# A planned attention-and-mixer kernel: transfers priced by packets, weights drawn forward, range check in two buffers

## The chip, the cores and the metric

The kernel runs on one core of one Trainium2 chip. The metric is the device time of one launch in microseconds, the median over several runs; lower is better. The engines are named as the profile names them: PE (matrix products, with PEld for loading their stationary side), DVE (vector), ACT (scalar), POOL and SP (which issues most DMAs).

## The reference

```
# attention: B, H, S, D = 4, 8, 768, 64; 16 centroids per head
q_n, k_n, c_n = (y / (norm(y) + 1e-6) for y in (q, k, centroids))
q_assign = argmax(q_n @ c_n.T);  k_assign = argmax(k_n @ c_n.T)
scores = where(q_assign == k_assign, q @ k.T / sqrt(D), -1e9)
attn_out = softmax(scores) @ v
# mixer on x = attn_out as (B, 768, 512); d_tok = 256, d_ch = 1536
h = relu(x.T @ w_tok1) @ w_tok2
u = x + h.T
out = u + relu(u @ w_ch1) @ w_ch2
```

q, k, v and the centroids are float32; the four weights come as float64, and the result is float32.

## The kernel before

The kernel first records every operation with its operands' places in one large SBUF tile (`arena`) and in PSUM (`ps`), and then a planner (`Program.run`, `Program.plan`) orders them. PE's operations keep the order in which they are recorded. For the other engines the planner keeps lists of operations whose predecessors are planned. At each step it takes, on the engine that can start soonest, the operation with the earliest due time among those that can start within `HOLD` of the first. Due times are worked backwards from PE's. Costs per engine are constants (`COST`, a cost given with `vec`), and a DMA occupies one shared bus for its bytes over `BUS` and lands `LAND` later. An operation with `after` isn't planned before that time. The order that comes out is written into each engine's queue; at run time each queue goes strictly in that order and waits on semaphores.

The work in PE's order:

- **Start.** Loads for the first pairs, the centroids' norm (`begin`), the first transposes by PE (`turn_qk`) and routing (`route`).
- **Attention.** 16 pairs of heads (`pair`). For each, `scores` makes 12 chunks of score products with a mask product added, ACT's exponential reads each chunk (line 1190), DVE adds the exponentials up (line 880), `sums` and `values` follow on PE, and `finish_x` transposes and scales the result on DVE (lines 1249 and 1263). `route` for the pair two ahead runs in between (DVE lines 1085 to 1090, ACT line 1094), and its mask goes through DRAM by two DMAs. The q and k of later pairs are turned by DMA transposes of 16-bit halves, with ACT copies on both sides (`part_qk`, `join_qk`, line 870).
- **Weights.** Beside attention the float64 weights are loaded in 31 pieces and rounded on DVE (`weight_round`, lines 1326, 1330, 1333, 1336 and a join on line 880). Piece n is not planned before `START + STEP * n`. The channel weights are combined for a seven-product scheme (two levels of it) and stored to DRAM (`wd1`, `wd2`) in 256-byte runs.
- **Token stage.** Seven-product forms of both token products (`token1`, `token2`). ACT copies halves for the transposes that bring x into u (`x_into_u`), and DVE adds PE's results.
- **Channel products.** `channel1` and `channel2`, each once for two batches (`grp` 0 and 1). Each calls `product` seven times, and each product reads seven weight tiles from DRAM into a ring of eight buffers, three matmuls to a tile. DVE or ACT copies take the results out of PSUM, and results go out by `send` and `store`.
- **Checks.** `weights_in_range` loads the raw weights again in 20 chunks of 768 KB into one buffer (`araw`), and ACT takes two sums of each (line 1863). `check` counts these, the softmax sums and the routing hits on DVE, adds them over partitions by one small matmul on PE, and makes a flag. `read_flag` loads the flag on every engine (line 1913). If it is not zero, `general_path` computes everything again; it is zero with these inputs.

A recorded operation carries the line of the helper that issues it: 841 for matmuls, 880 for two-operand adds, 860 for copies out of PSUM, 900 for DMAs.

Of the kernel before, what the change touches and what calls it, by code (L numbers as in the profile page):

```python
# [13 lines left out]
U32 = mybir.dt.uint32  # L14
ALU = mybir.AluOpType
ACT = mybir.ActivationFunctionType
# [14 lines left out]
HS = HJ * P  # L31
# [26 lines left out]
ISSUE = 0.63  # L58
BUS = 240e3
PASSES = 1  # L60
HOLD = {"DVE": 0.15}
WP = 768
NWP = (S * DTOK * 2 + DM * DCH * 2) // (P * WP)
LAND = 2.2
SWITCH = 0.1
SELF = 0.13
START, STEP = 14, 13


class Op:  # L70
    __slots__ = ("opts", "fn", "preds", "succs", "left", "ready", "end", "due", "seq", "eng", "lat", "bytes", "after", "port", "first_lat", "mode")


class Program:
# [7 lines left out]
    def __init__(self):  # L82
        self.ops, self.writer, self.readers = [], {}, {}

    def add(self, opts, fn, rd=(), wr=(), size=None, after=0.0, mode=None):

        o = Op()
        o.opts, o.fn, o.seq, o.succs, o.bytes, o.after = opts, fn, len(self.ops), [], 0, after
        o.lat, o.mode = 0.0, mode

        o.port = not any(type(k) is tuple and k[0] == "ps" for k in list(rd) + list(wr))
        if size:
            o.bytes = size[0] * (1.2 if size[1] < 512 else 1.0)
            o.lat = 5.0 + o.bytes / BUS
        o.first_lat = o.lat
        preds = set()
        for key in rd:
            if key in self.writer:
                preds.add(self.writer[key])
            self.readers.setdefault(key, []).append(o)  # L100
        for key in wr:
# [15 lines left out]
    def run(self):  # L117


        ops = self.ops  # L120

        free = 0.0
        for o in ops:
            c = min(o.opts.values())
            t = max([p.end + 0.15 + p.lat for p in o.preds], default=0.0)
            if "PE" in o.opts:
                t = max(t, free)
                free = t + c
            o.ready, o.end = t, t + c
        at = {o: o.ready for o in ops if "PE" in o.opts}  # L130
        total = max(o.end for o in ops)
        best = None
        for n in range(PASSES):

            for o in reversed(ops):
                c = min(o.opts.values())
                lat = o.first_lat
                if "PE" in o.opts:
                    o.due = at[o]
                else:  # L140
                    o.due = min([s.due - 0.15 - lat for s in o.succs], default=total) - c
            order, at, total = self.plan()
            if best is None or total < best[0]:
                best = (total, order)
        for o, e in best[1]:
            o.fn(e)

    def plan(self):
# [14 lines left out]
        while len(order) < len(ops):  # L163
            best = None
            for e in self.ENGINES:
# [5 lines left out]
                else:  # L171
# [548 lines left out]
def kernel(  # L720
# [27 lines left out]
    g = Program()  # L748
# [14 lines left out]
    at = 0  # L763

    def buf(kb, shape, dt=F32):
        return Buf(arena, int(kb * 256), shape, dt)
# [8 lines left out]
    cnt = Buf(arena, 352, [32])  # L775
    unsc = Buf(arena, 640, [2])
    low = Buf(arena, 644, [1])
    wsum = Buf(arena, 704, [2, NWP])
    araw = buf(75, [768, 2], U32)
    rcps = [Buf(arena, 384 + 32 * i, [2, NJ]) for i in range(2)]  # L780
    dall = Buf(arena, 448, [NP, 2, NJ])

# [7 lines left out]
    exs = [buf(48 + 6 * i, [2, S]) for i in range(6)] + [buf(96, [2, S])]  # L790
    es = [buf(84 + 6 * i, [2, S]) for i in range(2)]
    denT = buf(105, [HS])
    rt = [buf(106.5 + 1.5 * i, [HS]) for i in range(3)]

    qkr = buf(9, [2, 2, NJ, D])
# [39 lines left out]
    def bank(*i):  # L835
        return [("ps", n) for n in i]


    def mm(dst, lhsT, rhs, start, stop, cost, rd, wr, pos=None, tr=None):
        def fn(e):  # L840
            nc.tensor.matmul(  # L841
                dst, lhsT=lhsT, rhs=rhs, start=start, stop=stop, tile_position=pos,
                is_transpose=tr, skip_group_check=True,
            )

        return g.add({"PE": cost}, fn, rd, wr, mode=(lhsT.shape[0], lhsT.shape[1]))
# [43 lines left out]

        return g.add({e: cost(e, n) for e in engines}, fn, rd, wr)

    def vec(fn, c, rd, wr):
        return g.add({"DVE": c - 0.08}, lambda e: fn(), rd, wr)

    def dma(dst, src, rd, wr, kb, row, after=0.0, queue="SP"):

        q = {"SP": nc.sync, "ACT": nc.scalar, "POOL": nc.gpsimd}[queue]
        return g.add(
            {queue: ISSUE}, lambda e: q.dma_start(dst, src), rd, wr, (kb * 1024, row), after  # L900
        )

    def transpose(dst, src, rd, wr, kb):
        return g.add(
            {"SP": ISSUE}, lambda e: nc.sync.dma_start(dst, src, transpose=True), rd, wr,
            (1.3 * kb * 1024, 512),
        )


# [937 lines left out]
    def weights_in_range():  # L1847

        n = 0
        for w in (moe_w_tok1, moe_w_tok2, moe_w_ch1, moe_w_ch2):
            flat = w.rearrange("a b -> (a b)").rearrange("(p n) -> p n", p=P).bitcast(U32)
            for c in range(flat.shape[1] // (2 * WP)):
                dma(
                    araw.ap.rearrange("p n two -> p (n two)"),
                    flat[:, 2 * WP * c : 2 * WP * (c + 1)], [], araw.k(), 768, 6144, 430.0,
                )
                hi = araw.ap[:, :, 1].bitcast(F32)
                for i, (func, bias) in enumerate(((ACT.Square, 0.0), (ACT.Sign, low.ap))):  # L1860
                    g.add(
                        {"ACT": 0.9},
                        lambda e, i=i, func=func, bias=bias, n=n, hi=hi: nc.scalar.activation(  # L1863
                            out=hi, in_=hi, func=func, bias=bias, accum_out=wsum.ap[:, i, n : n + 1],
                        ),
                        araw.k() + low.k(), araw.k() + [("wsum", n)],
                    )
                n += 1

    def check():  # L1870
        n = NP * HJ * 4
        dv = dall.ap.rearrange("p m h j -> p (m h j)")
        ok = denT.ap[:, 0:n]
        rd = [("dall", m) for m in range(NP)]
        vec(lambda: nc.vector.tensor_scalar(
            out=ok, in0=dv, scalar1=SUM_LO, scalar2=None, op0=ALU.is_ge
        ), 0.3, rd, denT.k())
        vec(lambda: nc.vector.scalar_tensor_tensor(
            out=ok, in0=dv, scalar=SUM_HI, in1=ok, op0=ALU.is_le, op1=ALU.mult
        ), 0.3, rd + denT.k(), denT.k())  # L1880
        vec(lambda: nc.vector.reduce_sum(out=cnt.ap[:, 0:1], in_=ok, axis=AX.X), 0.3,
            denT.k(), cnt.k())
# [15 lines left out]
        vec(lambda: nc.vector.reduce_sum(  # L1898
            out=cnt.ap[:, 2:3], in_=wsum.ap, axis=AX.XY
        ), 0.2, wk, cnt.k())  # L1900
        mm(ps[0:32, 0, 0:3], ones.ap, cnt.ap[:, 0:3], True, True, 0.1,
           cnt.k() + ones.k(), bank(0), pos=(0, 0))
        tt(cnt.ap[0:1, 4:7], ps[0:1, 0, 0:3], want.ap[0:1], ALU.not_equal, 3,
           bank(0) + want.k(), cnt.k())
        vec(lambda: nc.vector.reduce_sum(
            out=cnt.ap[0:1, 7:8], in_=cnt.ap[0:1, 4:7], axis=AX.X
        ), 0.2, cnt.k(), cnt.k())
        vec(lambda: nc.vector.tensor_copy(
            out=cnt.ap[0:1, 8:9].bitcast(I32), in_=cnt.ap[0:1, 7:8]
        ), 0.2, cnt.k(), cnt.k())  # L1910
# [34 lines left out]
    left = [token2_sums(0)]  # L1945
# [17 lines left out]
    weights_in_range()  # L1963
    channel1(0)
    channel2(0)
    channel1(1)
    check()
    channel2(1)
    read_flag([])
    g.run()  # L1970
# [34 lines left out]
```

## Time and profile before

| | before |
|---|---|
| median of 3 runs | 803.17 us (802.9 to 803.7) |
| the profiled execution | 803.35 us, span 801.3 us, TensorE clock 0.998 |
| PE busy | 785.5 us, 98% of the span |
| DVE busy | 663.9 us, 83% |
| ACT busy | 468.0 us, 58% |
| POOL busy | 189.6 us, 24% |
| DMA | 264883 packets, 143.70 MB |

The span runs from the first to the last instruction; the profiled execution's own time has the launch around it. Busy times of matmuls are modelled and hold waits of a few tenths, so the distance between matmul records tells more than PE's share. The durations of single instructions overlap by up to a tenth of a microsecond with the next on their engine.

### The profile page before, as it was taken

To read this page: it belongs to the slowest core of one execution; us is meant where nothing else is said; L and a number is where in the kernel's file an instruction comes from. 1 tells how busy PE (TensorE), PEld (TensorE's weight loads), DVE (VectorE), ACT (ScalarE), POOL (GpSimd) and SP (SyncE) were. 2 spreads that over 40 slices of the span, in tenths; PEclk is the share of its full clock that TensorE was granted. 3 is DMA by queue.
4 is the path that set the end of the run, shared out by engine and by line. 5 is a ranking of instruction groups with operands and counts; after the bars stand their busy time and mean duration, and the time that the engine had idled before them with its cause. 6 is when DMAs were issued, how large, how long until landed. Compare 5 with 4: busy or idle time off the path is not lost.

```text
span 801.3 us, 15484 instructions
## 1 busy us (share of the span) xinstructions
PE 785.5 (98%) x6063; PEld 467.3 (58%) x6063; DVE 663.9 (83%) x863; ACT 468.0 (58%) x615; POOL 189.6 (24%) x185
## 2 busy tenths in 40 slices
PE   8999999999999999999999999999999999999995
PEld 5566666666666666544555555555555555555553
DVE  6888788999999999999998767899852677799962
ACT  5588888888888875699623235434537605401332
POOL 0000000000000000001255599700285289810000
PEclk9999999999999999999999999999999999999999
DMA  8466666998999875689967855557987943333765
GB/s 186 159 170 152 146 159 170 219 211 186 227 234 202 188 217 129 146 159 203 196 182 209 246 182 177 185 179 199 253 246 199 262 120 101 103 103 98 178 155 136
DMA packets 264883, 143.70 MB, mean 179 GB/s; under 512 B 184160, under 2 KB 260704, under 8 KB 264800
## 3 DMA queue, kind: packets, MB, share of 16 engines
q1 hardware_dynamic: 262432, 141.83, 70.0%
q8 instruction: 50, 0.82, 0.4%
q10 hardware_dynamic: 2368, 0.79, 0.4%
q14 instruction: 33, 0.27, 0.1%
HBM read 91.95 MB, written 28.61 MB: 150 GB/s over the span
## 4 chain that ended last, share of the span: by engine, by line
PE 83%; DVE 10%; ACT 4%; issue 2%; POOL 0%; DVEq 0%; POOLq 0%; ACTq 0%
PE ps L841 68%; PE ps L1207 15%; DVE arena L880 7%; ACT arena L870 2%; ACT arena L1190 1%; DVE arena L1330 1%; DVE arena L1333 0%; DVE arena L1263 0%; DVE arena L1336 0%; ACT arena L860 0%; ACT arena L887 0%; DVE arena L1326 0%; DVE arena L1249 0%; DVE arena L862 0%; DVE arena L1085 0%
## 5 line engine op out<-in xcount | busy, mean ns | idle before, releaser
L841 PE MATMUL ps<-arena 128*128 128x384 f32 (+5 forms) x2735 | 641.3, 462 | 7.9 <-DVE arena L862 2.1
L841 PEld LDWEIGHTS ps<-arena 128*128 128x128 f32 (+1 forms) x2351 | 341.5, 185 | 252.8 <-issue 58.6
L880 DVE TENSOR_TENSOR arena<-arena 128x256 f32<-128x256 f32 (+6 forms) x340 | 354.1, 1062 | 22.9 <-ACT arena L1190 14.2
L880 POOL TENSOR_TENSOR arena<-arena 128x384 f32<-128x384 f32 x179 | 188.9, 1085 | 514.8 <-DVE arena L880 390.9
L880 DVE TENSOR_TENSOR arena<-ps,arena 128x384 f32<-128x384 f32 (+3 forms) x227 | 189.1, 843 | 88.7 <-PE ps L841 85.2
L870 ACT COPY arena<-arena 128x768 uint16<-128x768 uint16 x223 | 191.4, 948 | 47.9 <-DMA arena<-arena 22.3
L1190 ACT ACTIVATE arena<-ps 128x768 f32<-128x768 f32 x192 | 153.0, 810 | 32.4 <-PE ps L841 30.7
L1207 PE MATMUL ps<-arena 128*32 128x192 f32 (+1 forms) x3328 | 151.1, 339 | 0.0
L1207 PEld LDWEIGHTS ps<-arena 128*32 128x32 f32 x3328 | 106.5, 110 | 48.0 <-issue 20.3
L860 ACT COPY arena<-ps 128x1152 f32<-128x1152 f32 (+2 forms) x42 | 30.8, 738 | 105.4 <-PE ps L841 105.4
L887 ACT ACTIVATE arena<-arena 128x1152 f32<-128x1152 f32 (+1 forms) x38 | 40.2, 1076 | 55.5 <-DVE arena L880 54.1
L1863 ACT ACTIVATE arena<-arena 128x768 f32<-128x768 f32 x40 | 38.8, 969 | 56.4 <-DMA arena<-in_moe_w_tok_dram 30.7
L841 PEld LDWEIGHTS <-arena 64*128 64x128 bf16 x384 | 19.2, 94 | 25.0 <-DVE arena L1117 0.6
L1094 ACT ACTIVATE arena<-arena 128x384 bf16<-128x384 f32 x16 | 11.3, 708 | 19.7 <-ACT arena L870 9.5
L1336 DVE SCALAR_TENSOR_TENSOR arena<-arena 128x512 f32<-128x512 uint32 (+1 forms) x31 | 21.2, 684 | 0.7
L1330 DVE SCALAR_TENSOR_TENSOR arena<-arena 128x512 uint32<-128x512 uint32 (+1 forms) x31 | 20.7, 669 | 0.8
L1263 DVE STREAM_TRANSPOSE arena<-ps 128x768 f32<-128x768 f32 x16 | 15.6, 975 | 1.1 <-PE ps L1207 1.0
L1333 DVE TENSOR_SCALAR arena<-arena 128x512 uint32<-128x512 uint32 (+1 forms) x31 | 14.2, 457 | 0.5
L1085 DVE STREAM_TRANSPOSE arena<-ps 128x384 f32<-128x384 f32 x16 | 9.3, 580 | 4.7 <-PE ps L841 4.6
L1326 DVE TENSOR_SCALAR arena<-arena 128x512 uint32<-128x512 uint32 (+1 forms) x31 | 12.5, 403 | 0.0
L1249 DVE STREAM_TRANSPOSE arena<-ps 128x384 f32<-128x384 f32 x16 | 9.2, 577 | 3.0 <-PE ps L1207 2.9
L1090 DVE STREAM_TRANSPOSE arena<-arena 128x384 f32<-128x384 f32 x16 | 9.3, 578 | 0.6
(58 smaller groups left out, 49.6 us busy)
## 6 DMA issues: line engine op xcount, KB each, us to landing
arena<-wd SPq DMA_DIRECT2D x196, 192.0 KB, 2.5
wd<-arena SPq DMA_DIRECT2D x84, 224.0 KB, 3.7
arena<-in_moe_w_ch_dram SPq DMA_DIRECT2D x48, 256.0 KB, 4.8
arena<-in_moe_w_ch_dram SPq DMA_DIRECT2D x16, 768.0 KB, 4.4
arena<-in_v_dram SPq DMA_DIRECT2D x16, 384.0 KB, 5.1
out_dram<-arena SPq DMA_DIRECT2D x14, 384.0 KB, 3.8
arena<-in_k_dram SPq DMA_DIRECT2D x13, 384.0 KB, 3.9
arena<-in_q_dram SPq DMA_DIRECT2D x13, 384.0 KB, 4.3
```

The lines of the kernel that those rows point to most:

```text
L841: nc.tensor.matmul(dst, lhsT=lhsT, rhs=rhs, start=start, stop=stop, tile_position=pos, is_transpose=tr, skip_group_check=True,)
L860: nc.scalar.copy(out=dst, in_=src)
L870: nc.scalar.copy(out=dst, in_=src)
L880: (nc.vector if e == "DVE" else nc.gpsimd).tensor_tensor(out=dst, in0=a, in1=b, op=op)
L887: nc.scalar.activation(out=dst, in_=src, func=ACT.Relu)
L1190: lambda e, ex=ex, s=s, u=u: nc.scalar.activation(out=ex.ap[:, :, u * HS : (u + 1) * HS], in_=ps[:, 2 * s : 2 * s + 2, 0:HS], func=ACT.Exp ...
L1207: nc.tensor.matmul(dst, lhsT=lhsT, rhs=rhs, start=start, stop=stop, tile_position=pos, skip_group_check=True,)
L1263: lambda: nc.vector.transpose(out=x.ap[:, :, cols].rearrange("p j (c d) -> p c j d", d=32), in_=ps[:, 6:8, 0:HS],),
L1330: vec(lambda: nc.vector.scalar_tensor_tensor(out=TT, in0=hi, scalar=0xC0000000, in1=hh, op0=ALU.bitwise_and, op1=ALU.bitwise_or), 0.14 + 0 ...
L1333: vec(lambda: nc.vector.tensor_scalar(out=hh, in0=TT, scalar1=0xFF800000, scalar2=None, op0=ALU.bitwise_and), f, T.k(), h.k())
L1336: vec(lambda: nc.vector.scalar_tensor_tensor(out=ll, in0=lo, scalar=float(2.0**-52), in1=hh.bitcast(F32), op0=ALU.mult, op1=ALU.mult,), 0. ...
L1863: lambda e, i=i, func=func, bias=bias, n=n, hi=hi: nc.scalar.activation(out=hi, in_=hi, func=func, bias=bias, accum_out=wsum.ap[:, i, n : ...
```

## The change

- A transfer's bytes on the planner's bus are now counted from its packets: 11 ns and 0.037 ns a byte for each run, over 16 DMA engines. DMA transposes are counted as 256-byte runs.
- ACT gets a `HOLD` of 0.2 us. DVE's stays at 0.15.
- `STEP` goes from 13 to 11 us, so piece n of the weights may be planned earlier.
- The range check of the weights alternates between two buffers (`araws`) and may begin at 418 us of the plan instead of 430.
- `check` uses a buffer of its own (`okb`) instead of `denT`, and is recorded ahead of `channel1(1)` instead of behind it, so that its matmul stands between the two groups in PE's order. The sum of the weights' counts gets a due time 20 us earlier (`early`).

```diff
-HOLD = {"DVE": 0.15}
+HOLD = {"DVE": 0.15, "ACT": 0.2}
...
-START, STEP = 14, 13
+START, STEP = 14, 11
...
         if size:
-            o.bytes = size[0] * (1.2 if size[1] < 512 else 1.0)
+            o.bytes = BUS * size[0] / size[1] * (11 + 0.037 * size[1]) / 16e3
             o.lat = 5.0 + o.bytes / BUS
...
-                    o.due = min([s.due - 0.15 - lat for s in o.succs], default=total) - c
+                    o.due = min([s.due - 0.15 - lat for s in o.succs], default=total) - c - o.early
...
-    araw = buf(75, [768, 2], U32)
+    araws = [buf(at, [768, 2], U32) for at in (75, 3)]
...
+    okb = buf(131.5, [HS])
...
     def transpose(dst, src, rd, wr, kb):
         return g.add(
             {"SP": ISSUE}, lambda e: nc.sync.dma_start(dst, src, transpose=True), rd, wr,
-            (1.3 * kb * 1024, 512),
+            (kb * 1024, 256),
         )
...
             for c in range(flat.shape[1] // (2 * WP)):
+                araw = araws[n % 2]
                 dma(
                     araw.ap.rearrange("p n two -> p (n two)"),
-                    flat[:, 2 * WP * c : 2 * WP * (c + 1)], [], araw.k(), 768, 6144, 430.0,
+                    flat[:, 2 * WP * c : 2 * WP * (c + 1)], [], araw.k(), 768, 6144, 418.0,
                 )
...
-        ok = denT.ap[:, 0:n]
+        ok = okb.ap[:, 0:n]
...
         vec(lambda: nc.vector.reduce_sum(
             out=cnt.ap[:, 2:3], in_=wsum.ap, axis=AX.XY
-        ), 0.2, wk, cnt.k())
+        ), 0.2, wk, cnt.k(), 20.0)
...
     weights_in_range()
     channel1(0)
     channel2(0)
+    check()
     channel1(1)
-    check()
     channel2(1)
     read_flag([])
```

More of the change, by code (lines that the diff above doesn't have):

```diff
@@ L66 @@
 SELF = 0.13
-START, STEP = 14, 13
+START, STEP = 14, 11
 class Op:
-    __slots__ = ("opts", "fn", "preds", "succs", "left", "ready", "end", "due", "seq", "eng", "lat", "bytes", "after", "port", "first_lat", "mode")
+    __slots__ = ("opts", "fn", "preds", "succs", "left", "ready", "end", "due", "seq", "eng", "lat", "bytes", "after", "port", "first_lat", "mode", "early")
 class Program:
@@ L83, in __init__, with add @@
         self.ops, self.writer, self.readers = [], {}, {}
-    def add(self, opts, fn, rd=(), wr=(), size=None, after=0.0, mode=None):
+    def add(self, opts, fn, rd=(), wr=(), size=None, after=0.0, mode=None, early=0.0):
         o = Op()
         o.opts, o.fn, o.seq, o.succs, o.bytes, o.after = opts, fn, len(self.ops), [], 0, after
-        o.lat, o.mode = 0.0, mode
+        o.lat, o.mode, o.early = 0.0, mode, early
         o.port = not any(type(k) is tuple and k[0] == "ps" for k in list(rd) + list(wr))
         if size:
-            o.bytes = size[0] * (1.2 if size[1] < 512 else 1.0)
+            o.bytes = BUS * size[0] / size[1] * (11 + 0.037 * size[1]) / 16e3
             o.lat = 5.0 + o.bytes / BUS
@@ L891, in relu, with vec @@
         return g.add({e: cost(e, n) for e in engines}, fn, rd, wr)
-    def vec(fn, c, rd, wr):
-        return g.add({"DVE": c - 0.08}, lambda e: fn(), rd, wr)
+    def vec(fn, c, rd, wr, early=0.0):
+        return g.add({"DVE": c - 0.08}, lambda e: fn(), rd, wr, early=early)
     def dma(dst, src, rd, wr, kb, row, after=0.0, queue="SP"):
@@ L1876, in check @@
             out=ok, in0=dv, scalar1=SUM_LO, scalar2=None, op0=ALU.is_ge
-        ), 0.3, rd, denT.k())
+        ), 0.3, rd, okb.k())
         vec(lambda: nc.vector.scalar_tensor_tensor(
             out=ok, in0=dv, scalar=SUM_HI, in1=ok, op0=ALU.is_le, op1=ALU.mult
-        ), 0.3, rd + denT.k(), denT.k())
+        ), 0.3, rd + okb.k(), okb.k())
         vec(lambda: nc.vector.reduce_sum(out=cnt.ap[:, 0:1], in_=ok, axis=AX.X), 0.3,
-            denT.k(), cnt.k())
+            okb.k(), cnt.k())
         vec(lambda: nc.vector.reduce_sum(out=cnt.ap[:, 10:11], in_=hits.ap[:, 0:NP], axis=AX.X), 0.2,
```

## The prediction

> **What bounds the kernel now.** I read the page's engine totals first, then busy time by stage, then the groups and waits of the stage that looked worst.
>
> ```profile
> span 801.3 us, 15484 instructions
> PE 785.5 (98%) x6063; PEld 467.3 (58%) x6063; DVE 663.9 (83%) x863; ACT 468.0 (58%) x615; POOL 189.6 (24%) x185
> PE 83%; DVE 10%; ACT 4%; issue 2%; POOL 0%; DVEq 0%; POOLq 0%; ACTq 0%
> ```
>
> TensorE is the bound, so the change can only win back time in which PE waits. A busy PE row includes stretched matmuls, so I count records against a full rate. The chain of waits shows that rate, and the period of one head pair in attention:
>
> ```profile
> 117.65 9.89 PE ps L841 x72
> 137.41 9.89 PE ps L841 x72
> ...
> 420.06 300.70 PE ps L841 x932
> ```
>
> The half with the channel products issues a 384-wide record every 300.70/932 = 0.323 us with hardly a gap; a 512-wide one should take 4/3 of that, 0.430 us. A head pair repeats every 137.41 - 117.65 = 19.76 us. Busy time by stage (columns: stretch, length, busy time and count of PE, PEld, DVE, ACT, POOL, then clock, DMA share, GB/s), and the token stage's matmul groups and waits:
>
> ```profile
> 180.00:200.00 20.00, 20.00 (x294) 12.54 (x292) 19.15 (x29) 17.38 (x23) 0.00 (x0) 1.00 0.84 189
> 220.00:240.00 20.00, 20.00 (x292) 12.44 (x290) 19.17 (x28) 17.38 (x23) 0.00 (x0) 1.00 0.95 232
> 333.60:421.00 87.40, 85.60 (x233) 42.62 (x230) 84.16 (x148) 61.39 (x77) 18.64 (x18) 1.00 0.86 183
> 421.00:621.00 200.00, 200.00 (x621) 117.42 (x620) 149.41 (x147) 88.21 (x129) 106.57 (x100) 1.00 0.72 207
> 720.00:760.00 40.00, 39.91 (x123) 22.68 (x121) 39.19 (x43) 9.25 (x13) 0.00 (x0) 1.00 0.58 141
> ...
> L841 PE MATMUL ps<-arena 128*128 128x384 f32 x145 | 49.0, 491 | 1.4 <-DVE arena L880 1.3
> L841 PE MATMUL ps<-arena 128*128 128x512 f32 x84 | 37.3, 598 | 0.4 <-ACT arena L860 0.2
> ...
> PEld ps L841 <- DVE arena L880: 6.8, 11, 1.2
> PEld ps L841 <- ACT arena L860: 2.6, 3, 1.0
> ```
>
> In the token stage (333.6 to 421) 145 x 0.323 + 84 x 0.430 = 82.9 us of matmuls took 87.4 us: PE loses 4.5 us there. DVE is busy 84.16 of 87.40 us, and of PE's weight-load waits 6.8 us are for DVE and 2.6 for ACT. In attention PE holds its period although DVE is at 19.2 of 20 us. So what can be won lies in the token stage, a little in the first 40 us, and a little at 720 to 760, where DVE is again full.
>
> **The change part by part.** Since all engines' order comes from the planner, I compare the order of the instructions before and after. PE's own order is unchanged but for the check's matmul and the flag load. All sums are against the profiled execution's 803.35 us (span 801.3); the median 803.17 is 0.02% below it, which I do not correct for.
>
> (1) STEP 11 for 13 draws the weights' rounding forward. One channel piece is four steps and a join, and its share of the product sums:
>
> ```profile
> L880 DVE TENSOR_TENSOR arena<-arena 128x448 f32<-128x448 f32 x48 | 29.7, 632 | 0.2
> L880 DVE TENSOR_TENSOR arena<-arena 128x512 f32<-128x512 f32 x35 | 24.5, 706 | 1.5 <-ACT arena L870 0.9
> L880 DVE TENSOR_TENSOR arena<-arena 128x256 f32<-128x256 f32 x48 | 19.4, 430 | 0.5
> L1336 DVE SCALAR_TENSOR_TENSOR arena<-arena 128x512 f32<-128x512 uint32 x27 | 19.0, 703 | 0.6
> L1330 DVE SCALAR_TENSOR_TENSOR arena<-arena 128x512 uint32<-128x512 uint32 x27 | 18.5, 686 | 0.7
> L1333 DVE TENSOR_SCALAR arena<-arena 128x512 uint32<-128x512 uint32 x27 | 12.8, 474 | 0.4
> L1326 DVE TENSOR_SCALAR arena<-arena 128x512 uint32<-128x512 uint32 x27 | 11.1, 413 | 0.0
> ```
>
> That is 0.41 + 0.69 + 0.47 + 0.70 + 0.71 = 2.98 us, and 2 x 0.43 + 2 x 0.63 = 2.12 us of sums: 5.1 us. By the order, 7 pieces stand behind the last pair's finish (L1263) before and 5 after, and none of the 5 in the channel products' time, where two stood. Two pieces, 10.2 us, leave DVE's queue between that finish and the first channel products; if nearly all of it is the token stage's, DVE has some 75 us to do there, not 84.2. DVE's part of the 4.5 us lost, by the waits 6.8/(6.8 + 2.6), is 3.2 us. I take four fifths, **-2.6 us**, since the middle of the stage still holds pieces; bounds 0 (ACT's copies are next late) and -3.8 (all but 0.7).
>
> The price is in attention. With the rows' durations (overlap with the next instruction taken off), DVE's work between two finishes of pairs 5 to 13 was 15.4 to 19.2 us and becomes 19.0, 19.0, 19.5, 19.2, 19.3, 20.0, 19.3, 19.8, 19.6: 19.4 on average, against 19.76. DVE keeps up by 0.4 us a pair; and the planner, which takes the earliest due step first, leaves the steps that free PE's banks ahead of rounding. I take **0**, up to +2 if it slips.
>
> The DMAs move too. The counting by packets (11 ns + 0.037 ns a byte) makes large rows cheaper and 256-byte transposes about 8% cheaper in the plan, so loads are planned to land earlier. In attention the weights' loads and stores come 13/11 as often, over a share of 0.84 to 0.95 already; the busiest pairs will be close to 1. [...]
>
> (2) The start is reordered by the new transfer prices.
>
> ```profile
> 20.23 0.71 ACT L1094 ACTIVATE arena<-arena 128x384 bf16<-128x384 f32 x1
> 21.77 0.30 PEld L841 LDWEIGHTS ps<-arena 64*128 64x128 f32 x4 [0.57 <-ACT arena L1190]
> ...
> 36.69 0.35 DVE arena L1333
> 37.06 0.69 DVE arena L1336
> 37.75 0.59 DVE arena L1085
> 38.38 10.10 PE ps L841 x72
> ```
>
> L1094 of pair 1 (0.71 us and its read) sat among pair 0's exponentials and PE waited behind it; it now comes after the tenth, when PE needs no more than two: about -0.35. At 36.69 two rounding steps stood ahead of L1085, which frees the bank that pair 1 starts in; now they come after it, and the third PSUM copy is ACT's. L1085 then starts when route's matmuls end, some 0.5 us sooner. Together **-0.85**, bounds -0.2 and -1.3 (the mask copies, shuffled too, could give some back).
>
> (3) The range check of the weights is drawn together.
>
> ```profile
> L1863 ACT ACTIVATE arena<-arena x40: 904/968/1031, 434.9 to 636.1; 128x768 f32<-128x768 f32 x40
> L1863 ACT ACTIVATION_READ_ACCUMULATOR arena<-arena x40: 182/190/198, 435.7 to 637.0; 128x1 f32 x40
> L860 ACT COPY arena<-ps 128x1152 f32<-128x1152 f32 x15 | 16.8, 1118 | 36.7 <-PE ps L841 36.7
> arena<-in_moe_w_ch_dram SPq DMA_DIRECT2D x16, 768.0 KB, 4.4
> ```
>
> A chunk costs ACT 2 x (0.97 + 0.19) = 2.3 us. In the order its 20 chunks stand over some 85 us of PE's matmuls instead of 200. ACT has room, but a range step ahead of a PSUM copy makes 1.16 + 1.12 = 2.28 us where a product step has 6 x 0.323 = 1.94: the second of two such copies is 0.7 us late, where its bank leaves 1.94 - 1.12 = 0.8 us less the handing over, an estimated 0.5. **+0.4**, bounds 0 and +1.5. On SP a chunk's load now waits for the chunk two earlier, with ring loads queued behind it; the ring is eight loads deep, some 15 us of PE work, so I price that at nothing; without that cover each wait would be PE's.
>
> (4) The counts. check's early sums go to its own buffer (okb) and run at the start of the channel products, off DVE's full stretch at 720 to 760; the matmul and the flag come at the seam of the two groups, where DVE is light. Every engine still loads the flag, so its queue still waits there.
>
> ```profile
> PEld ps L841 <- DVE arena L1908: 0.8, 1, 0.8
> ```
>
> The flag's weight-load wait was 0.8 us, of which a quieter DVE can save a part. I take **-0.3**, bounds -0.8 and +0.3. ACT's HOLD only lets a due step pass another by 0.2 us: nothing. The tail's order is the same except that one store is issued earlier: nothing.
>
> Sum: -2.6 + 0 - 0.85 + 0.4 - 0.3 = -3.35; 803.35 - 3.35 = **800.0 us**.
>
> **The rivals.** *ACT holds the token stage.* ACT has 61.4 us to do there, whose copies also free PE's banks. If DVE's relief wins only 1.0 us: 801.6. The 2.6 against 6.8 us of waits speak against.
>
> *No gain in all.* The token stage wins nothing and the copies cost 1.5: 803.35 - 0.85 + 1.5 - 0.3 = 803.7, no change. For it: PE's loss is spread over many small waits.
>
> *DVE becomes the bound in attention: slower.* Place: pairs 5 to 13. Each pair rounds 1.8 pieces; if each waits for its load because DMA is full, 0.4/1.8 = 0.22 us a piece eats DVE's room. At 0.6 us a piece each pair takes 19.4 + 1.1 = 20.5 us, +0.7, nine times: +6.3, and the token stage starts as late on DVE as before. 803.35 + 6.3 - 0.85 + 0.4 - 0.3 = 808.9. Against: at a share of 0.95 PE's period did not move.
>
> *PE waits for the counts: slower.* The check's matmul now stands 588 records, 190 us, behind the start of the channel products, at about 596. At the old pace, (636.1 - 434.9)/20 = 10.1 us a chunk, the last sum would be ready at about 625: +29 us, 829. It decides from 8.5 us a chunk; with 2.3 us of ACT and 4.4 of landing even one buffer would do, so this is unlikely. [...]
>
> **How the numbers follow.** Forecast 0.66, ACT rival 0.14, no gain 0.10, DVE bound 0.07, counts 0.03. The range reaches from -5.2 (most terms near their good ends), 798.2, to 802.8, which takes in the ACT rival and the forecast with its costs at the bad ends; the last three and the edges are left out. 0.2% is 1.6 us, about what can be told here: faster is below 801.7, which holds the forecast's greater part and half the ACT rival: 0.76. Same 0.13, slower 0.11.
>
> **What would show it.** In the profile after: the pair period still 19.76 us; pair 1 starting near 37.5; in the token stage PE's loss down from 4.5 to about 2 us, with the DVE share near 85%; range steps (L1863) all between about 423 and 515; ACT's PSUM copies among them followed by short PE waits; the check's matmul without a wait at about 595. A pair period above 19.8, a DVE idle before L1326 put down to a DMA, or a PE gap of microseconds at the check would make the prediction wrong.

## The result and the profile after

| | before | after |
|---|---|---|
| median | 803.17 us (7 runs, 802.55 to 803.70) | 800.18 us (7 runs, 799.38 to 800.95) |
| ratio of the times | | 0.9962, 95% interval 0.9950 to 0.9973 |
| the profiled execution | 803.35 us, span 801.3 us | 799.38 us, span 797.6 us |

The change saves 3.0 us; 800.0 was forecast. The parts are another matter. The page of the changed kernel, its totals and the shares of its chain:

```profile
span 797.6 us, 15467 instructions
PE 783.8 (98%) x6063; PEld 466.9 (59%) x6063; DVE 659.4 (83%) x861; ACT 469.8 (59%) x618; POOL 188.8 (24%) x184
...
PE 82%; DVE 11%; ACT 4%; issue 2%; ACTq 0%; DVEq 0%
```

PE is the bound as before. (Line numbers are one or two higher: 841 is now 842, 880 is 881, 1863 is 1865.) The chain of the changed kernel at the start, in attention and at its end, and busy time by stage (columns as in the prediction):

```profile
37.15 0.59 DVE arena L1086
37.74 0.04 issue
37.79 9.96 PE ps L842 x72
...
97.15 9.89 PE ps L842 x72
...
116.91 9.89 PE ps L842 x72
...
792.22 0.56 DVE arena L863
```

```profile
180.00:200.00 20.00, 20.00 (x292) 12.47 (x290) 19.28 (x30) 17.38 (x23) 0.00 (x0) 1.00 1.02 224
240.00:260.00 20.00, 20.00 (x294) 12.38 (x290) 19.27 (x28) 17.39 (x23) 0.00 (x0) 1.00 1.00 236
333.60:421.00 87.40, 85.14 (x231) 42.47 (x230) 82.24 (x142) 60.90 (x77) 21.16 (x20) 1.00 0.76 163
421.00:621.00 200.00, 200.00 (x622) 117.39 (x621) 138.96 (x138) 101.17 (x148) 102.17 (x97) 1.00 0.71 210
```

Pair 1 starts at 37.79 instead of 38.38 us, the pair period is still 116.91 - 97.15 = 19.76 us, and PE keeps it with DVE at 19.3 of 20 us and a DMA share of 1.00 to 1.02. But the token stage shows the failed step: DVE is busy 82.24 us there, not some 75, and its waits have not shrunk:

```profile
PEld ps L842 <- DVE arena L881: 7.7, 13, 1.5
PEld ps L842 <- ACT arena L861: 1.5, 2, 1.2
```

PE's waits for DVE are 7.7 us where they were 6.8. Where the rounding stood tells why DVE's time fell so little. The last of the 31 pieces begins in before, then in after:

```profile
427.45 0.41 DVE L1326 TENSOR_SCALAR arena<-arena 128x512 uint32<-128x512 uint32 x1
```

```profile
394.01 0.41 DVE L1327 TENSOR_SCALAR arena<-arena 128x512 uint32<-128x512 uint32 x1
```

So the last of the seven pieces that stood behind the last pair's finish in before lay wholly behind 421 us, in the channel products' time. The four rounding steps (L1326, L1330, L1333, L1336) took 13.7 us of DVE inside the window and 3.6 us from 421 to 440; in after they take 11.1 us and nothing. The two pieces that left thus had little more than one piece's steps in the token stage.

To place the gain I compare the start of the same matmul in both traces, the kernels' records being matched by their place in PE's order. The first loads land up to 0.9 us apart from run to run of one and the same program, so each difference counts from the 54th record on (10 us into the span). In this measure two traces with the same plan agree to 0.02 us (after and after_pad). Differences from the kernel before, in us, at places of PE's order named by their time in before; the last column is what is left of the span behind the start of PE's last matmul. The check's own matmul, which the change moves, is left out of the matching. The kernels below the second row are those of the experiments:

| kernel | 45 us | 330 | 420 | 440 | 560 | 660 | 700 | 793 | tail |
|---|---|---|---|---|---|---|---|---|---|
| before | 0 | 0 | 0 | 0 | 0 | 0 | 0 | 0 | 8.18 |
| after | -0.38 | -0.38 | -0.17 | -0.17 | -0.22 | +0.13 | -0.22 | -0.86 | 5.65 |
| before_pad | 0.00 | 0.00 | 0.00 | 0.00 | +0.01 | +0.01 | +0.01 | 0.00 | 5.69 |
| after_pad | -0.38 | -0.38 | -0.16 | -0.16 | -0.21 | +0.15 | -0.21 | -0.84 | 7.97 |
| step_alone | -0.09 | +6.54 | +6.14 | +6.14 | +6.02 | +6.46 | +6.46 | +5.91 | 5.77 |
| prices_alone | -0.09 | -0.10 | +0.25 | +0.52 | +0.36 | +0.36 | +0.36 | -0.22 | 5.81 |
| step_prices | -0.09 | -0.09 | +0.65 | +0.65 | +0.52 | +0.97 | +0.97 | +0.40 | 7.69 |
| check_alone | 0.00 | 0.00 | +0.01 | +0.01 | +10.90 | +35.48 | +35.12 | +34.49 | 7.75 |
| range_alone | 0.00 | 0.00 | +0.01 | +0.01 | +0.22 | +0.22 | +0.22 | -0.37 | 7.78 |
| after_step13 | -0.38 | -0.38 | +0.83 | +1.09 | +12.58 | +13.42 | +13.07 | +12.43 | 5.68 |
| step13_late | -0.38 | -0.38 | +0.80 | +1.06 | +0.91 | +1.26 | +0.91 | +0.27 | 5.70 |
| after_port | -0.38 | -0.38 | -0.17 | -0.17 | +7.31 | +8.15 | +7.79 | +7.16 | 6.88 |
| step12_late | -0.38 | -0.38 | -0.24 | -0.05 | -0.20 | +0.15 | -0.20 | -0.85 | 5.86 |
| token_free | -0.38 | -0.38 | -0.76 | -0.86 | -0.90 | -0.54 | -0.90 | -1.53 | 5.75 |

So PE's last matmul starts 0.86 us earlier, and the tail behind it is 8.18 - 5.65 = 2.53 us shorter: three quarters of the 3.39 us by which the two profiles differ behind the first loads, in a part that I had priced at nothing. SP's closing semaphore steps of both kernels, first and last start at the end of each row:

```profile
L2000 SPq EVENT_SEMAPHORE  x10: 17/28/28, 797.6 to 801.2; - x10
```

```profile
L2002 SPq EVENT_SEMAPHORE  x10: 17/28/28, 796.2 to 797.5; - x10
```

The same ten steps, 0.03 us each, span 3.6 us before and 1.3 us after. In the records of before, SP stands still for 2.30 us between the fourth (797.87) and the fifth (800.20); all that the DMA engines move from 797 to 802 us are five packets of the two queues marked instruction (for which engines, the view doesn't say):

```profile
DMA packets 5, 0.05 MB, mean 10 GB/s; under 512 B 0, under 2 KB 0, under 8 KB 0
q14 instruction: 4, 0.03, 1.8%
q8 instruction: 1, 0.02, 1.5%
```

### The profile page after: what moved, and what is told of

Its sections match the earlier page's. It is cut to its first block, busy times and chain, and to the rows that moved or that the text cites. A ratio compares the mean times of both kernels' runs of the same rounds, so it can differ in the third digit from the quotient of the medians.

```text
span 797.6 us, 15467 instructions
## 1 busy us (share of the span) xinstructions
PE 783.8 (98%) x6063; PEld 466.9 (59%) x6063; DVE 659.4 (83%) x861; ACT 469.8 (59%) x618; POOL 188.8 (24%) x184
## 4 chain that ended last, share of the span: by engine, by line
PE 82%; DVE 11%; ACT 4%; issue 2%; ACTq 0%; DVEq 0%
PE ps L842 65%; PE ps L1208 17%; DVE arena L881 9%; ACT arena L871 3%; ACT arena L861 1%; ACT arena L888 0%; DVE arena L863 0%; DVE arena L1264 0%; DVE arena L1337 0%; ACTq L901 0%; ACT L980 0%; ACT arena L1191 0%; DVE arena L1334 0%; DVE arena L1331 0%; DVE arena L1086 0%
## 5 line engine op out<-in xcount | busy, mean ns | idle before, releaser
L881 DVE TENSOR_TENSOR arena<-arena 128x1536 f32<-128x1536 f32 (+6 forms) x341 | 354.8, 1063 | 19.8 <-ACT arena L1191 9.0
L881 POOL TENSOR_TENSOR arena<-arena 128x384 f32<-128x384 f32 x178 | 188.1, 1086 | 516.5 <-DVE arena L881 382.4
L881 DVE TENSOR_TENSOR arena<-ps,arena 128x384 f32<-128x384 f32 (+3 forms) x227 | 189.3, 844 | 100.2 <-PE ps L842 90.4
L861 ACT COPY arena<-ps 128x1152 f32<-128x1152 f32 (+2 forms) x45 | 32.8, 738 | 133.7 <-PE ps L842 125.2
L1327 DVE TENSOR_SCALAR arena<-arena 128x512 uint32<-128x512 uint32 (+1 forms) x31 | 12.6, 406 | 0.3 <-DMA arena<-in_moe_w_ch_dram 0.3
L1334 DVE TENSOR_SCALAR arena<-arena 128x512 uint32<-128x512 uint32 (+1 forms) x31 | 12.3, 409 | 0.4
```

Of the source, the lines that this page charges most:

```text
L861: nc.scalar.copy(out=dst, in_=src)
L881: (nc.vector if e == "DVE" else nc.gpsimd).tensor_tensor(out=dst, in0=a, in1=b, op=op)
L1327: vec(lambda: nc.vector.tensor_scalar(out=hh, in0=hi, scalar1=0x07FFFFFF, scalar2=3, op0=ALU.bitwise_and, op1=ALU.logical_shift_left,), f, ...
```

## The experiments

Theories at the outset: the forecast's (weights drawn forward relieve DVE in the token stage); a layout theory (SP's program is 11 instructions shorter, and SP's gap hangs on the place of its closing steps in that program); a store theory (the tail is shorter because a store is issued earlier). In all of the texts "place" is the number of SP's instructions that stand ahead in its program, general_path's 369 among them.

**Only the layout.** One line of general_path, which isn't entered, is repeated, in the kernel before 24 times more and in the changed one 11 times:

```diff
-        nc.sync.dma_start(cen, centroids.rearrange("h c d -> (h c) d"))
+        for _ in range(25):    # 12 in the changed kernel
+            nc.sync.dma_start(cen, centroids.rearrange("h c d -> (h c) d"))
```

> The kernel before, with 24 more loads on SP inside general_path, which is never entered: what every engine executes is the same, only SP's closing instructions move from places 1357-1369 of its program to 1381-1393. Layout theory (the 2.3 us in which SP stands still between the fourth and fifth of its closing semaphore steps is a wait for a block of its program, whose border lies at place 1361): the gap goes, the tail behind PE's last matmul falls from 8.2 to about 5.9 us, and the time from 803.17 to about 800.9 us. Store theory (the tail is shorter in the changed kernel because one store is issued earlier): the tail stays 8.2 us and the time 803.2. The forecast's theory (the gain is PE's, not the tail's) also gives 803.2.

> The changed kernel, with 11 more loads on SP inside general_path, so that SP's closing instructions stand at places 1357-1369 as they did before the change. Layout theory: the 2.3 us gap comes back behind the fourth closing semaphore step, the tail grows from 5.65 to about 8 us, and the time from 800.2 to about 802.5 us. Store theory and the forecast's theory: no change, tail 5.65 us, 800.2 us.

Measured: before_pad 801.15 us, ratio 0.9977 (0.9968 to 0.9986); after_pad 802.08 us, ratio 0.9986 (0.9977 to 0.9995). PE runs as in the unpadded kernels (table). SP's closing steps, first before_pad and then after_pad:

```profile
L2001 SPq EVENT_SEMAPHORE  x10: 17/28/28, 797.2 to 798.5; - x10
```

```profile
L2003 SPq EVENT_SEMAPHORE  x10: 17/28/28, 797.3 to 800.7; - x10
```

The gap goes from the one (1.3 us) and comes to the other (3.4 us), 2.12 us behind the fourth step. Nothing that is executed was changed, so the place of SP's closing steps in its program makes the gap, and the store theory falls. That SP waits there for a block of its program, with a border at place 1361, was a guess: no run shows what it waits for, and from 798.6 to 800.2 us in before no DMA packet moves at all. By medians the gap is worth 803.17 - 800.18 - (802.93 - 802.08) = 2.1 us of the 3.0 (802.93 is the kernel before beside after_pad), and 1.8 us by before_pad; the tails in the profiles say 2.3 to 2.5.

The other kernels' closing steps move with the length of SP's queue, and the gap stays where the program's place is 1361: behind the fourth step in before and after_pad, the eighth in range_alone (1.99 us), the ninth in check_alone (1.87), the twelfth in after_port (1.66). The nine others, whose closing steps end below 1361 or begin above it, have none of SP's own. One of them, step_prices, has its gap on ACT instead (1.95 us, and the others wait for it), whose two closing DRAINs lie 2.8 us apart, where 1.0 is usual:

```profile
L2000 ACTq DRAIN  x2: 8/72/135, 797.7 to 800.5; - x2
```

ACT's queue is the longest of all there (864 records against 844 to 859 in the others); whether ACT's gap hangs on a place in its program too wasn't tested. I had reckoned with SP's alone.

**STEP 11 and the transfer prices, each alone and together.** To the kernel before:

```diff
-START, STEP = 14, 13
+START, STEP = 14, 11                     # step_alone, step_prices
-            o.bytes = size[0] * (1.2 if size[1] < 512 else 1.0)
+            o.bytes = BUS * size[0] / size[1] * (11 + 0.037 * size[1]) / 16e3   # prices_alone, step_prices
-            (1.3 * kb * 1024, 512),
+            (kb * 1024, 256),                # transposes; prices_alone, step_prices
```

> The kernel before with STEP 11 for 13 alone. SP's closing instructions come to 1345-1357. The forecast's theory: PE loses about 2 us in the token stage instead of 4.6, nothing elsewhere; 803.17 - 2.6 = 800.6 us with the tail as before. Layout theory: PE's loss in the token stage stays at 4 to 5 us, PE's last matmul starts within 0.4 us of before (793.1), and all of the gain is the tail's: 8.2 down to about 5.9 us, 800.9 us. The two times are near each other; the profile's split between PE's last matmul and the tail tells them apart.

> The kernel before with the transfer prices alone (bytes by packets, transposes as 256-byte runs), STEP still 13. SP's closing instructions come to 1340-1352. The forecast's theory: pair 1 starts 0.7 to 0.85 us sooner and the rest is as before, 802.4 us with the tail of 8.2 us. Layout theory: the same 0.7 us at the start and, without the closing gap, 2.3 us at the tail: about 800.2 us.

> The kernel before with STEP 11 and the transfer prices, without ACT's HOLD, the two buffers and the moved counts. Theory A (the prices are what keeps STEP 11 from making PE wait for the routing mask's load behind the crowded weight transfers, which cost 6.5 us in STEP 11 alone): no loss between 260 and 330 us, pair 1 about 0.1 us earlier as with the prices alone, the rest of the start's gain (0.3 us) missing since it is HOLD's, and with no closing gap 800.3 to 801.3 us. Theory B (HOLD or another part does that): the mask waits return, 805 to 808 us.

Measured: step_alone 807.67 us, ratio 1.0057 (1.0043 to 1.0070); prices_alone 801.05, 0.9976 (0.9967 to 0.9986); step_prices 802.99, 1.0003 (0.9994 to 1.0012). No theory had step_alone slower, and prices_alone shows 0.09 us at the start where both theories had 0.7. The waits of step_alone from 250 to 334 us, its records on PE, and on SP the order of issue ahead of them:

```profile
PEld L841 <- DMA arena<-wdm: 3.0, 1, 3.0
PE ps L841 <- DMA arena<-wdm: 2.3, 1, 2.3
```

```profile
296.29 0.92 PE L841 MATMUL ps<-arena 64*128 64x384 f32 x4
299.55 2.23 PE L841 MATMUL ps<-arena 64*128 64x384 bf16 x10 [2.34 <-DMA arena<-wdm]
...
289.10 2.12 SPq L900 DMA_DIRECT2D arena<-in_moe_w_ch_dram  x2
291.26 0.62 SPq L900 DMA_DIRECT2D arena<-wdt  x1
292.29 0.36 SPq L900 DMA_DIRECT2D wd<-arena  x1
292.71 2.30 SPq L900 DMA_DIRECT2D arena<-wdm  x2
```

The routing mask comes back from DRAM (`wdm`) too late: its loads stand on SP behind the crowded weight transfers and are issued at 292.71 us, when PE needs them near 297. The wait makes PE 2.5 us later, and 1.9 us more go in the next 4.5 us, with a lower granted clock (the first number behind the POOL column, below: 0.91 from 300 to 320 us). Another 1.3 go near 322, where PE waits for DVE (L1249); whether that follows from the first wait isn't shown. The rest, 0.9 us, goes in smaller steps before and after. The stretch behind the wait:

```profile
300.00:320.00 20.00, 20.00 (x277) 13.91 (x276) 19.52 (x27) 9.70 (x12) 0.00 (x0) 0.91 0.66 163
```

In step_prices, STEP 11 again, the same loads are issued at 284.14 us and the loss is nil (-0.09 at 330), as in the changed kernel (283.92):

```profile
284.14 1.56 SPq L900 DMA_DIRECT2D arena<-wdm  x2
```

So the prices keep STEP 11 from costing 6.5 us; theory A holds for that. It was wrong on the time, 802.99 against 800.3 to 801.3, by the gap on ACT and by +0.7 us in the token stage, where STEP alone gave -0.4 and the prices alone +0.35. In step_alone, though, PE enters that stage 6.5 us late, and DVE had that time to work ahead: its rounding steps there take 6.7 us, not 11 to 14.

**The counts and the range check, each alone.** To the kernel before, the check's part of the diff (okb, the early due time, check ahead of channel1(1)) in one, and the two buffers with 418 in the other.

```diff
+    check()                                   # check_alone
     channel1(1)
-    check()
...
-    araw = buf(75, [768, 2], U32)
+    araws = [buf(at, [768, 2], U32) for at in (75, 3)]    # range_alone, with 418.0 for 430.0
```

> The kernel before with the counts alone moved (okb, the early due time, check ahead of channel1(1)); STEP 13, the old prices and the old range check stay. Theory of the traces: of the changed kernel's PE gain some 0.6 us behind 700 us is this part's, so PE's last matmul comes 0.4 to 0.8 us earlier against the first score product than in the kernel before, and nothing moves ahead of 560 us. Forecast's theory: 0.3 us. Layout theory for the tail: SP's closing instructions stand at places 1352-1364, the border at 1361 lies behind the ninth of them, so a gap of about 2 us stands there instead of behind the fourth, and the time is about 802.5 us; without the layout theory 802.5 to 802.9 too, with the gap's place unchanged or no gap. Rival (PE waits for the counts, since the range check is not drawn together here): at the old pace of 10.1 us a chunk the last sum comes at about 636 us where the matmul stands at about 596, so PE would stall some 40 us.

> The kernel before with the two buffers and the 418 us of the range check alone. Forecast's theory: ACT's range steps ahead of PSUM copies cost +0.4 us between 423 and 520 us. Theory of the traces: they cost nothing there, at most 0.3 us between 560 and 600 us, where loads and copies meet. Either way the time is 802.9 to 803.3 us. Layout theory for the tail: closing instructions at places 1353-1365, a gap of about 2 us behind the eighth of them.

Measured: check_alone 837.45 us, ratio 1.0425 (1.0412 to 1.0439); range_alone 802.22, 0.9990 (0.9982 to 0.9999), 0.7 us under what both theories gave: PE is 0.37 us earlier, by its gain behind 720 us, and the tail 0.4 us shorter. The records of check_alone on PE and DVE:

```profile
483.55 104.93 PE L842 MATMUL ps<-arena 128*128 128x384 f32 x318 [8.54 <-DVE arena L881]
633.87 6.61 PE L842 MATMUL ps<-arena 128*32 128x3 f32 x15 [21.39 <-DVE arena L1899]
...
472.45 9.78 DVE L1879 SCALAR_TENSOR_TENSOR arena<-arena 128x192 f32<-128x192 f32 x1
```

Two stalls. The second is the rival of the prediction that had 0.03: the counts' matmul waits 21.4 us for the last range sums, which at the old pace come at 632. What prevents it in the changed kernel is the range check drawn together, here of check_alone, of after and of range_alone, whose last sum comes 50 us ahead of the place of the counts' matmul near 600 us:

```profile
L1864 ACT ACTIVATE arena<-arena x40: 875/954/1030, 435.3 to 632.3; 128x768 f32<-128x768 f32 x40
```

```profile
L1865 ACT ACTIVATE arena<-arena x40: 900/967/1036, 426.7 to 512.1; 128x768 f32<-128x768 f32 x40
```

```profile
L1864 ACT ACTIVATE arena<-arena x40: 892/969/1032, 428.8 to 549.5; 128x768 f32<-128x768 f32 x40
```

So an edit that I costed at +0.4 us is the condition of the next one. The first stall, at 475 us, nobody expected: a DVE step of the counts that takes 0.36 us in the changed kernel (423.33) takes 9.78 here.

**STEP 13 in the changed kernel, and the counts' place.** after_step13 has only STEP 13; the two behind it say when the first of the counts' steps may be planned:

```diff
         vec(lambda: nc.vector.tensor_scalar(
             out=ok, in0=dv, scalar1=SUM_LO, scalar2=None, op0=ALU.is_ge
-        ), 0.3, rd, okb.k())
+        ), 0.3, rd, okb.k(), after=530.0)     # step13_late (STEP 13); after_port: 462.0 (STEP 11)
```

> The changed kernel with STEP back at 13. Forecast's theory: the weights drawn forward are worth 2.6 us in the token stage, so PE's loss there grows to about 7 us and the time to about 802.8 us. Theory of the traces: STEP is worth 0.4 us there at most and nothing elsewhere once the transfer prices are right, so PE's last matmul moves by under 0.6 us and the time stays at 800.0 to 800.8 us (closing instructions at 1347-1359, no gap).

> The changed kernel with STEP 13, in which 13 us appeared, and with one more edit: the first of the counts' DVE steps may not be planned before 530 us, so the two-input step on okb can't fall into GpSimd's unbroken run of adds (455 to 482 us). Port theory (that step, 0.36 us alone, stood 9.8 us because a DVE step with two SBUF inputs gets no turn while GpSimd's adds follow each other without a gap): the step takes about 0.4 us again, PE's 8.6 us wait at 475 us is gone, and the time falls from 813.3 to 801.5-802.5 us (PE about 1 us behind the changed kernel at 440 us, no closing gap on SP). Rival (STEP 13 itself brings the 13 us, by pieces that come too late for the channel products): the stall at 475 us stays and the time stays at 812 to 814 us.

> The changed kernel, STEP 11, with one edit: the first of the counts' DVE steps may not be planned before 462 us, so that they leave their place at 423 us and the two-input step comes to stand amid GpSimd's run of adds. Port theory: the step takes about 10 us instead of 0.36, PE waits 8 to 9 us near 475 to 485 us, and the time is 810 to 814 us. Rival (the stall belongs to STEP 13): no stall and 799.5 to 801 us. Layout theory for the tail: SP's closing instructions at places 1349-1361, so a gap of about 2 us, if any, right ahead of the last of them.

Measured: after_step13 813.28 us, ratio 1.0103 (1.0067 to 1.0138), which neither of its theories had (six of seven runs 811.99 to 813.77, one 802.55); step13_late 801.66, ratio 0.9984 (0.9975 to 0.9993); after_port 808.90, 1.0083 (1.0069 to 1.0096), 1.1 us under the port theory's range, as the step that stood there took 6.85 us and not 10. Timelines of DVE and GpSimd in after_step13, then in after_port, and in step13_late:

```profile
472.69 9.84 DVE L1880 SCALAR_TENSOR_TENSOR arena<-arena 128x192 f32<-128x192 f32 x1
482.46 1.34 DVE L881 TENSOR_TENSOR arena<-ps,arena 128x1152 f32<-128x1152 f32 x1
...
455.44 26.88 POOL L881 TENSOR_TENSOR arena<-arena 128x384 f32<-128x384 f32 x28 [2.25 <-DVE arena L881]
```

```profile
477.23 6.85 DVE L1877 TENSOR_SCALAR arena<-arena 128x192 f32<-128x192 f32 x1
...
454.17 29.79 POOL L881 TENSOR_TENSOR arena<-arena 128x384 f32<-128x384 f32 x31 [2.26 <-DVE arena L881]
```

```profile
555.39 0.35 DVE L1880 SCALAR_TENSOR_TENSOR arena<-arena 128x192 f32<-128x192 f32 x1
...
455.66 38.55 POOL L881 TENSOR_TENSOR arena<-arena 128x384 f32<-128x384 f32 x40 [2.25 <-DVE arena L881]
```

In both slow kernels the DVE step ends within 0.3 us of the last of GpSimd's adds (455.44 + 26.88 = 482.32, 454.17 + 29.79 = 483.96), and so it does in check_alone (482.23 and 482.01). Undisturbed, in step13_late, the run goes on for 40 adds, to 494.2 us; so the runs of 28 and 31 probably ended only because PE and DVE stood and GpSimd had nothing left to add. Moved out of that run it is short and the stall is gone, at STEP 13; moved into it, the stall is there at STEP 11, though with the one-input step ahead of the two-input one that I had named. PE pays because DVE frees its banks next (L881, reading PSUM). So neither STEP nor late weights make the 12 us. What let one run of after_step13 pass without it isn't known, no trace having caught it.

**The token stage without the rounding.**

```diff
+        if npiece <= 26:      # counted from 1: the four steps of the last five pieces are left out
             vec(lambda: nc.vector.tensor_scalar(
                 out=hh, in0=hi, scalar1=0x07FFFFFF, scalar2=3,
```

> The changed kernel without the four rounding steps of the last five weight pieces (the join stays), so the values of those pieces are not computed: 5 x 2.27 = 11.4 us less work for DVE from the last pair's finish to the first channel products. Forecast's theory (DVE's load as a whole makes PE's waits there; two pieces are worth 2.6 us): PE's loss of 4.85 us in the token stage falls to about 1 us and the time to about 796.5 us. Rival (PE waits on single steps, product sums and ACT's copies behind their own predecessors, and DVE's load is not what holds them): the loss stays above 4 us and the time within 0.8 us of 800.2. Between the two: rounding steps stand right ahead of the sums at the stalls, and those alone go, 1.5 to 2.5 us.

Measured: 799.41 us, ratio 0.9954 (0.9942 to 0.9967). Its token stage, and its waits from 375 to 421 us beside those of after:

```profile
333.60:421.00 87.40, 85.65 (x233) 42.98 (x232) 73.17 (x127) 60.82 (x77) 22.14 (x21) 1.00 0.79 166
...
PEld ps L842 <- DVE arena L881: 4.5, 9, 0.6
```

```profile
PEld ps L842 <- DVE arena L881: 7.0, 12, 1.5
```

DVE is down to 73.2 of 87.4 us, 84%, about what I took for the changed kernel, and PE gains 0.6 us at 420 (-0.17 to -0.76), not 3. From 375 on rounding was what PE waited for (its three largest losses in after, 1.06, 0.64 and 0.34 us near 400, 407 and 419, are 0.17 or nothing); but the new plan has two new losses of 1.0 us near 368 and 372. Since the plan changes with the kernel, the worth of a single step can't be read from this run; that the load as a whole isn't worth 3 us can. My expectation between the two theories, 1.5 to 2.5 us, was too high in all.

**A sturdier version.** The changed kernel with STEP 12 and the first of the counts' steps not before 530 us.

> A version that could be better than both: the changed kernel with STEP 12 and the counts' first DVE step not before 530 us, clear of GpSimd's run whatever the plan. Theory of the traces: up to the end of attention as the changed kernel (pair 1 to 0.05 us), in the token stage between 0.4 us better and 1 us worse, since single steps and not DVE's load decide there, no stall at 475 us, no closing gap: 799.5 to 801.5 us. Forecast's theory: each step of STEP is worth 1.3 us in the token stage, so about 801.5 us. A stall of 8 us or more would speak against the port theory.

Measured: 799.82 us, ratio 0.9965 (0.9952 to 0.9979). It beats the kernel before as the changed one does and can't be told from that one (0.9962); its merit is that the counts stand where GpSimd is idle (from 554.3 us).

## Why the prediction came out right

The total was right by luck: a term of -2.6 that did not come was made up by one of -2.1 that I had priced at nothing, and the other terms' errors nearly cancel.

| step | forecast | measured | by |
|---|---|---|---|
| token stage, relief of DVE | -2.6 | +0.2 | table, 330 to 420 us |
| attention | 0 | 0.0 | table, 45 to 330 us |
| start | -0.85 | -0.38 | table, 10 to 45 us |
| range steps ahead of copies | +0.4 | 0.0 | table, 420 to 560 us |
| counts and flag | -0.3 | 0.0 (+0.35 near 600 us, -0.35 near 695) | table, 560 to 700 us |
| behind 700 us, with any new plan | 0 | -0.64 | table, 700 to 793 us |
| HOLD of ACT | 0 | about -0.3, within the start | the start's rows, by exclusion |
| tail | 0 | -2.1 | after_pad, medians |

The sum of PE's steps is -0.38 + 0.21 - 0.05 + 0.35 - 0.35 - 0.64 = -0.86; with -2.1 it gives the measured -3.0.

**The failed step** is "DVE has some 75 us to do there", and with it the rule of three from waits to load. I took both pieces that leave DVE's queue as the token stage's, though by my own reading of the order two pieces stood in the channel products' time. The window lost 2.7 us of rounding, not 10.2 us of work, and DVE's time in it went from 84.2 to 82.2 us. And token_free shows that even at 73 us PE loses about 4.3 us (4.85 us in after, by the starts of its matmuls, less the 0.6): so the waits hang on where single steps stand, and DVE's load as a whole is no measure of them. Plans with other STEPs and prices moved that stage by -0.4 (step_alone) to +1.2 us (step13_late). STEP 11 for 13 was worth -0.4 us there by itself (with PE 6.5 us late), +0.4 beside the prices alone (step_prices against prices_alone) and -1.0 in the whole change (after against step13_late): it has no price of its own. Here the rival of no gain in the token stage was right.

**The start.** Of the 0.74 us between the two profiles' attention 0.36 are the first loads, which vary by themselves. The prices or STEP alone give -0.09; every kernel with ACT's HOLD gives -0.38 and none without it does. HOLD alone wasn't run, but of the change nothing else is common to these kernels and lacking in step_prices that acts ahead of 45 us (check and range alone: 0.00). So "ACT's HOLD: nothing" was very likely wrong.

**Attention.** Nothing was lost, as forecast, but I had named the wrong cover. What stands between STEP 11 and a loss isn't the 0.4 us of DVE's room but the prices: without them the mask's loads come late (+6.5 us). The rival of a DMA that is full was near: crowded weight transfers did cost in step_alone, but by the mask's load and not by DVE's rounding. The crowding by itself cost nothing: at a DMA share of 1.00 to 1.02 PE lost nothing in after, and in step_alone it was the order of issue that cost.

**The counts and the range steps.** The -0.35 us between 660 and 700 is the counts', but no gain. PE loses 0.35 us near 600, where their matmul now stands, and gets as much back near 695, where it stood; each kernel with check moved and its matmul not delayed has both at just these two places (step13_late +0.35 and -0.35), and none of the others has either there. The 0.6 us from 720 on is nobody's: prices_alone and range_alone have it as well (-0.58, -0.59), so every new plan avoided what the old one lost there. The +0.4 for range steps ahead of copies did not come: from 420 to 560 us, around their time of 426.7 to 513, after moves by -0.05 us. The rival "PE waits for the counts" is real without the range check drawn together; its size, forecast at 29 us, was a wait of 21.4 and 2.1 us more at a lower clock.

**The tail.** "One store is issued earlier: nothing" was right of the store, and blind to the length of SP's program, which the change makes 11 instructions shorter.

## What to carry to other kernels

Compare the same instruction in both traces, from a point behind the first loads, before explaining a gain of a few microseconds: it shows to 0.02 us where time was won, and here it moved over two thirds of the gain out of the parts that had been argued for. Follow it to the instruction, too: a loss and a gain of the same size, 95 us apart, were one matmul that had moved. A busy engine's share was no price for a wait here (DVE at 73 of 87 us, and PE still lost 4.3): what counted was which steps stood ahead of the one PE waited for. And work taken out of a queue relieved only the stage in which it stood (two pieces of 10.2 us gone, 2.7 us less rounding in the token stage). And edits that cost nothing may be what others stand on: prices for STEP 11, two buffers for the earlier counts, and a place clear of GpSimd's adds for two steps of 0.3 us.

## What the runs showed of the hardware

**SP's gap at the program's end.** In before, 3.2 us pass between the closing branch (L1972) and the next instruction on DVE's queue, 2.9 on ACT's and 3.2 on SP's, and eight packets of the queues marked instruction move from 792 to 798 us. SP stands still 1.7 to 2.3 us more where place 1361 falls among the last 13 of the 21 instructions behind the branch (2.30 in before, 2.12 in after_pad, 1.99 in range_alone, 1.87 in check_alone, 1.66 in after_port); ACT did so once, for 1.95 us (step_prices). What the engines wait for isn't shown. By the medians the gap cost 1.8 to 2.1 us of this kernel.

**DVE's steps amid GpSimd's adds.** A DVE step from SBUF to SBUF of 0.25 us (L1877) or 0.36 us (L1880), as they take in after at 423 us, took 6.85 us amid 31 adds of GpSimd (L1877 in after_port) and 9.84 amid 28 (L1880 in after_step13), while DVE's adds that read PSUM took 1.36 us among them as elsewhere. The step ended within 0.3 us of the last of the adds, and not after one of them (1.0 us). It is not each such step: in after_step13 L1877 took 0.29 us at 459.15 us, amid the same 28 adds. The port theory's two SBUF inputs weren't needed, L1877 having one; why the step waits isn't shown.

**The clock after a wait.** Behind PE's wait of 2.3 us in step_alone 1.9 us more went (granted clock 0.91 from 300 to 320 us). Behind the waits of 5.7 to 8.6 us in after_port, check_alone and after_step13 it was 1.8, 2.2 and 2.9 us (clock 0.80 and 0.76 from 480 to 500 us in the last two), and 2.1 behind the 21.4 us in check_alone: 384-wide matmuls start every 0.64 us instead of 0.32 for 4 to 6 us, and then at the old pace again. PE's records in after_port ahead of its wait and behind it:

```profile
469.63 10.16 PE L842 MATMUL ps<-arena 128*128 128x384 f32 x31
485.45 9.71 PE L842 MATMUL ps<-arena 128*128 128x384 f32 x24 [5.66 <-issue]
```
